# Float32 products for four units instead of eight, a fourth place for arriving weights, and x's first maximum spread in another bank

## The chip, the cores and the metric

The kernel runs on one core of a Trainium2 chip. The metric is the time of one execution on the device in microseconds (us), from the first to the last of its work; lower is better. The core's engines that appear here are TensorE (PE for its products, PEld for its weight loads), VectorE (DVE), ScalarE (ACT), GpSimd (POOL) and SyncE (SP), which in this kernel issues the transfers between HBM and the core's memory. PE writes its results into PSUM, in banks of 128 x 512 float32.

## The reference

Clustered attention over 4 batches, 8 heads, 768 positions and 64 columns a head, followed by a two-layer MLP on the result:

```python
q_assign = argmax(einsum('bhsd,hcd->bhsc', q_n, c_n))     # 16 clusters a head
k_assign = argmax(einsum('bhsd,hcd->bhsc', k_n, c_n))
scores = q @ k.T / sqrt(D), or -1e9 where q_assign != k_assign
attn = exp(scores - max(scores)); attn = attn / (sum(attn) + 1e-9)
x = (attn @ v) laid out as 3072 tokens x 512
h = x @ w_in                                              # 512 x 2048
g = s * relu(h)**2 + b
out = g @ w_out                                           # 2048 x 512
```

Everything comes and leaves in float32. The kernel does most products in float16, with a value split in a high and a low half (hi, lo) and three products added up.

## The kernel before

**Attention** is cut into 192 units, numbered in the order (b, c, hp, t, h): batch, a chunk of 256 positions, a pair of heads, a tile of 128 queries and a head of the pair. Four units share a chunk and pair of heads. For a unit, PE makes 128 x 768 scores (scores, L465), DVE takes the maximum (L475), ACT the exponential (exps, L482 and L485). The result p has to be transposed before it can be multiplied with the values. Up to unit 15 (TURN = 16) PE does this, three 128 x 128 pieces at a time (L509), into two PSUM banks that are called `turned` and that later hold the MLP's sums; from unit 16 on a transfer does it. Units 0 to 7 (RAW = 8) are copied out of the banks in float32, one half by DVE (L122) and one by ACT (L120), and multiplied with the values in float32 (L531). Units 8 to 15 are split: ACT writes the high part in float16 (L514), DVE subtracts it for the low part (L515), and 18 float16 products per unit follow (L536 to L538), in which the values are split too (prep_v). Units from 16 on are split before their transpose and multiplied at L563 to L565.

**x.** After four units, finish_x (L577) writes x split in two halves and has it transposed by a transfer. After the 16 units of a chunk of 256 tokens it takes x's maximum: DVE over the columns (L595), then allmax, in which PE spreads the 128 partitions' maxima over a bank (L98) and DVE reduces them (L99). The bank is the one of the tag m, of which there is one; the cluster products of later queries (`pq`, L396), and the values of the first 16 units (`px`), use it too.

**The weights.** w_in and w_out come as 32 pieces of 512 KB (fetch, L83 and L86), alternately wi and wo. They land in a tile with the tag stage, of which there are three. rebase (ACT, L204) and narrow (DVE, L208 and L209) turn the raw bits of a piece into a float32 tile and so free its place. bound (ACT, L216 or L218, with PE and DVE for wi) takes sums that bound the products. weights() holds these steps at a fixed distance: in round i, bound of piece i-3, rebase and narrow of i-2, fetch of i. When all pieces have been bounded, two scales follow (finish_w_in, finish_w_out), and wsplit makes float16 pairs of all weights (ACT L266, DVE L268), one step of the MLP after the other.

**The MLP** is 192 steps (b, c, ft): for each chunk of 256 tokens, 16 blocks of 128 hidden columns. A step is mlp_in (12 products, L620), mlp_relu (ACT: r, L627; g's high half, L629; the square, L630), mlp_gl (POOL, L635: g's low half) and mlp_out (6 products, L647). mlp_start makes a chunk's scales from x's maximum in seven small DVE operations (L602 to L611), the first L627 needs them. In the program the steps run 21 units behind the attention (LAG = 21).

**What sets the order.** The program is written unit by unit, with helpers that advance a step at a time. Each engine's order is then made by a scheduler, which puts an instruction where its own estimate and the priorities allow; `tc.high_priority(offset=300)` (first_of_all) lets the instructions under it move ahead, and is used for the first 20 units. On the chip each engine then runs its instructions in that order, and waits for each one's inputs and buffers.

Of the kernel before, what the change touches and what calls it, by code (L numbers as in the profile page):

```python
# [8 lines left out]
F16 = mybir.dt.float16  # L9
# [9 lines left out]
P = 128  # L19
# [7 lines left out]
def tile_cluster_attention_mlp(ctx, tc, q, k, v, cent, w_in, w_out, s_in, b_in, out):  # L27
# [15 lines left out]
    LAG = 21  # L43
    BIGN = 11

    RAW = 8
    TURN = 16
    URGENT = 20

# [43 lines left out]

    def allmax(dst, src, name, bank="m"):
        n = src.shape[1]
        pm = (ps_m if bank == "m" else ps_h).tile([P, 512], F32, tag=bank, name=f"am_{name}")
        for j in range(n):
            nc.tensor.matmul(pm[:, j * P : (j + 1) * P], src[:, j : j + 1].broadcast_to([P, P]), identb, start=True, stop=True)  # L98
        V.tensor_reduce(dst, pm[:, : n * P].rearrange("p (n q) -> p n q", q=P), axis=AX.X, op=ALU.max)  # L99
# [14 lines left out]
    G.tensor_copy(identb, ident)  # L114
    ones16 = const([P, P], F16, "ones16")
    G.memset(ones16, 1.0)

    def copy(eng, dst, src):
        if eng is A:
# [46 lines left out]
    wo = {}  # L166
    WSP = {}

    def weight_tile(name):
        return cp.tile([P, KT, P], F32, tag="w", name=name, bufs=2 * NF + 1)  # L170
    w1 = const([P, NF], F32, "w1")
# [18 lines left out]
    def fetch(p):  # L190
        ft = p // 2
        if p % 2 == 0:
            w = wi[ft] = weight_tile(f"wi{ft}")
            src = w_in.bitcast(I32)[:, ft * 2 * P : (ft + 1) * 2 * P].rearrange("(t p) f -> p t f", p=P)
        else:
            w = wo[ft] = weight_tile(f"wo{ft}")
            src = w_out.bitcast(I32)[ft * P : (ft + 1) * P, :].rearrange("p (a f) -> p a f", a=KT)
        st = sb.tile([P, KT, P, 2], I32, tag="stage", name=f"wst_{p}", bufs=3)
        load(st.rearrange("p a f w -> p a (f w)"), src)
        return {"w": w, "st": st, "p": p, "ft": ft}  # L200

    def rebase(d):
        hw = d["st"][:, :, :, 1].bitcast(F32)
        A.activation(d["w"], hw, AF.Prelu, scale=2.0 ** -112, alpha=-(2.0 ** 32))  # L204

    def narrow(d):
        c = d["w"].bitcast(I32)
        V.tensor_scalar(c, c, 3, None, op0=ALU.logical_shift_left)  # L208
        V.scalar_tensor_tensor(c.bitcast(U32), d["st"][:, :, :, 0].bitcast(U32), 29, c.bitcast(U32),  # L209
                               op0=ALU.logical_shift_right, op1=ALU.bitwise_or)  # L210
# [16 lines left out]

    def weights():
        live = {}
        for i in range(2 * NF + 3):  # L230
            if 0 <= i - 3:
                bound(live[i - 3])
                narrowed[0] += 1
            if 0 <= i - 2 < 2 * NF:
                rebase(live[i - 2])
                narrow(live[i - 2])
            if i < 2 * NF:
                live[i] = fetch(i)
            if i < 2 * NF + 2:
                yield  # L240

    def finish_w_in():
# [164 lines left out]
    def prep_v(b):  # L407
        vm = sb.tile([P, 8], F32, tag="vm", name=f"vm_{b}", bufs=2)
        VM[b] = vm
        vns = []  # L410
        for hp in range(NP):
            vn = sb.tile([P, 2, T, D], F32, tag="kv", name=f"vn_{b}_{hp}", bufs=5)
            load(vn, v[b, 2 * hp : 2 * hp + 2].rearrange("h (p t) d -> p h t d", t=T), False)
            vns.append(vn)
            if b == 0:
                VN[hp] = vn
            yield
        if b:
            yield from until(START[b][3])
        for hp in range(NP):  # L420
            absmax(vm[:, hp : hp + 1], vns[hp].rearrange("p h t d -> p (h t d)"))
            if hp < NP - 1:
                yield
        vc = columns(1, f"v{b}")
        V.tensor_reduce(vc, vm[:, 0:NP], axis=AX.X, op=ALU.max)
        if b:
            yield
        allmax(vm[:, 5:6], vc, f"v{b}")
        yield
        floor2(V, vm[:, 6:7], vm[:, 5:6])  # L430
        inverse2(V, vm[:, 7:8], vm[:, 6:7], 0)
        V.tensor_scalar(vm[:, 7:8], vm[:, 7:8], 2.0 ** 13, None, op0=ALU.mult)
        V.tensor_scalar(vm[:, 6:7], vm[:, 6:7], 2.0 ** -19, None, op0=ALU.mult)
        for hp in range(NP):
            vh = sb.tile([P, 2, T, D + 2], F16, tag="vh", name=f"vh_{b}_{hp}", bufs=5)
            vl = sb.tile([P, 2, T, D], F16, tag="vl", name=f"vl_{b}_{hp}", bufs=5)
            VS[(b, hp)] = (vh, vl)
            G.memset(vh[:, :, :, D:], 1.0)
            yield from split(vh[:, :, :, :D], vl, vns[hp], vm[:, 7:8], False)
            if hp < NP - 1:  # L440
                yield
                if b > 0:
                    yield from until(48 * b - 8 + 4 * hp)
# [133 lines left out]
    def finish_x(g):  # L577
        b, c, hp = units[4 * g][:3]
        xs = XT.pop(g)
        if 4 * g < RAW:  # L580
            A.activation(xs, xs, AF.Copy, scale=VM[0][:, 7:8])
        if hp == 0:
            XM[(b, c)] = sb.tile([P, 8], F32, tag="xm", name=f"xm_{g}", bufs=4)
        xn = sb.tile([P, CT, 2, 2, D], F16, tag="xn", name=f"xn_{g}", bufs=1)
        A.activation(xn[:, :, 0], xs, AF.Copy)
        absmax(XM[(b, c)][:, hp : hp + 1], xs.rearrange("p t h d -> p (t h d)"))
        yield
        G.tensor_tensor(xn[:, :, 1], xs, xn[:, :, 0], op=ALU.subtract)
        x = sb.tile([P, CT, 2, P], F16, tag="x", name=f"x_{g}", bufs=9)
        XS[(b, c, hp)] = x  # L590
        nc.sync.dma_start_transpose(x.rearrange("p t e q -> p (t e) q"), xn.rearrange("p t e h d -> p (t e h d)"))
        if hp == NP - 1:
            xm = XM[(b, c)]
            xc = columns(1, f"x{g}")
            V.tensor_reduce(xc, xm[:, 0:NP], axis=AX.X, op=ALU.max)  # L595
            allmax(xm[:, 5:6], xc, f"x{g}")


    MS = {}
# [23 lines left out]
    def mlp_relu(b, c, ft):  # L623
        n = f"{b}_{c}_{ft}"
        ph = GS[(b, c, ft)]
        r = sb.tile([P, CW], F32, tag="r", name=f"r_{n}", bufs=2)
        A.activation(r, ph[:, :CW], AF.Relu, scale=MS[(b, c)][0])  # L627
        g = sb.tile([P, 2, CW], F16, tag="g", name=f"g_{n}", bufs=4)
        A.activation(g[:, 0, :], r, AF.Square)  # L629
        A.activation(r, r, AF.Square)  # L630
        GS[(b, c, ft)] = (r, g)
# [54 lines left out]
        at(LAG - 4 + ft, wsplit(ft))  # L686
    wgen = weights()

    def first_of_all(k):
        return tc.high_priority(offset=300) if k < URGENT else nullcontext()  # L690

    def run(gen):
        for _ in gen:
            pass
# [41 lines left out]
    with behind(last_turn[0], *last_split):  # L736
        some(first_v, 1)
        sv = scalar_in(s_in, "sv")
        bv = scalar_in(b_in, "bv")
        some(wgen, 3)  # L740
    run(first_k[0])
    run(first_q[0])
    run(first_k[1])
# [2 lines left out]
    while i < NU + 8 or i - LAG < NS + 4:  # L746
# [21 lines left out]
                exps(i)  # L768
        if 0 <= m < NS:
            if steps[m][2] == 0:  # L770
                mlp_start(*steps[m][:2])
            mlp_in(*steps[m])
            mlp_relu(*steps[m])
        if 0 <= i - 1 < NU:
# [38 lines left out]
```

## Time and profile before

| | us |
|---|---|
| median of three runs | 953.33 (951.72 to 954.87) |
| the profiled execution | 951.04 |
| its span, first to last instruction | 949.3 |
| PE busy | 835.3 (88%) |
| ACT busy | 713.9 (75%) |
| DVE busy | 639.7 (67%) |
| POOL busy | 546.4 (58%) |

All times of single instructions are from the profiled execution, counted from the start of its span. The program falls into stages: up to about 36 us the first keys and queries are prepared, from about 24 to 122 us the weights arrive beside the first units, to about 161 us they are split, and from about 165 us on the MLP's steps run between the units. The units end near 880 us.

### The profile page before, as it was taken

What the parts mean: (1) busy time and instruction counts of PE and PEld (TensorE: products, weight loads), DVE (VectorE), ACT (ScalarE), POOL (GpSimd) and SP (SyncE); (2) the same over time, 40 slices, a digit from 0 to 9 for tenths busy, and PEclk for the clock granted to TensorE, in tenths of its full rate; (3) what the DMA queues carried; (4) which work ended last, traced back from release to release, by engine and by line L of the source; (5) the groups of instructions that cost most, each with busy time, mean ns of one, the idle gap of its engine ahead of it and who ended that gap; (6) DMA issues with size and microseconds to landing.
All of it is one profiled execution on the core that took longest, in us unless ns stands there. A gap on an engine that the chain in (4) does not pass through costs nothing. (4 is left out here: it accounts for less than half of the span.)

```text
span 949.3 us, 22900 instructions
## 1 busy us (share of the span) xinstructions
PE 835.3 (88%) x8673; PEld 586.3 (62%) x8673; DVE 639.7 (67%) x1680; ACT 713.9 (75%) x1406; POOL 546.4 (58%) x580
## 2 busy tenths in 40 slices
PE   0567566988999898999998999999999999999997
PEld 0356343656566566777676666666776667777664
DVE  7797888999577767667876766776686567654100
ACT  3476766777587777888887978887888788888443
POOL 3010114577576666778687667776776666676321
PEclk9967575899999899999999999999999999999999
DMA  6888813778787897969778877888978768575300
GB/s 174 219 215 242 225 38 78 181 141 145 160 157 146 178 200 132 181 150 180 157 173 151 198 181 147 160 146 185 180 160 167 145 129 165 125 161 114 46 23 23
DMA packets 437759, 144.25 MB, mean 152 GB/s; under 512 B 405392, under 2 KB 434064, under 8 KB 437648
## 3 DMA queue, kind: packets, MB, share of 16 engines
q1 hardware_dynamic: 437648, 142.78, 71.6%
q8 instruction: 68, 1.11, 0.5%
q14 instruction: 43, 0.35, 0.1%
HBM read 35.69 MB, written 6.29 MB: 44 GB/s over the span
## 5 line engine op out<-in xcount | busy, mean ns | idle before, releaser
L517 POOL TENSOR_TENSOR ph<-p,ph 128x768 f16<-128x768 f32 x176 | 298.5, 1696 | 92.8 <-ACT ph L120 53.8
L647 PE MATMUL acc<-wos,g 128*128 128x512 f16 x1152 | 299.8, 381 | 5.1 <-POOL g L635 4.6
L620 PE MATMUL h<-x,wis 128*128 128x256 f16 x2304 | 290.5, 275 | 5.1 <-DMA x<-xn 3.3
L620 PEld LDWEIGHTS <-wis 128*128 128x128 f16 x2304 | 220.5, 98 | 53.7 <-issue 6.7
L635 POOL TENSOR_TENSOR g<-r,g 128x256 f16<-128x256 f32 x192 | 135.0, 704 | 120.8 <-ACT r L630 100.7
L485 ACT ACTIVATE p<-sc,ssm,qsm 128x768 f32<-128x768 f32 x192 | 188.3, 981 | 2.1
L475 DVE TENSOR_REDUCE ssm<-sc 128x1 f32<-128x768 f32 x192 | 181.9, 948 | 6.9 <-PE sc L465 6.9
L647 PEld LDWEIGHTS <-g 128*128 128x128 f16 x1152 | 102.7, 98 | 82.3 <-POOL g L635 7.5
L627 ACT ACTIVATE r<-h,cf 128x256 f32<-128x256 f32 x192 | 89.6, 467 | 77.2 <-PE h L620 63.4
L120 ACT ACTIVATE ph<-p 128x768 f16<-128x768 f32 x164 | 136.4, 832 | 0.6
L482 ACT ACTIVATE ssm<-ssm,lift,qsm 128x1 f32<-128x1 f32 x192 | 73.0, 380 | 70.5 <-DVE ssm L475 68.9
L563 PE MATMUL sc<-vh,PT 128*128 128x65 f16 x1032 | 118.1, 196 | 7.0 <-DMA PT<-ph 6.8
L565 PE MATMUL sc<-vh,PT 128*128 128x65 f16 x1032 | 120.5, 194 | 0.0
L564 PE MATMUL sc<-vl,PT 128*128 128x64 f16 x1032 | 119.4, 193 | 0.0
L563 PEld LDWEIGHTS <-PT 128*128 128x128 f16 x1056 | 99.4, 98 | 26.4 <-DMA PT<-ph 13.7
L465 PE MATMUL sc<-KA,QA 128*128 128x384 f16 x384 | 99.7, 342 | 16.3 <-ACT p L485 12.8
L564 PEld LDWEIGHTS <-PT 128*128 128x128 f16 x1056 | 98.9, 100 | 12.0 <-issue 0.7
L465 PE MATMUL sc<-KB,QB 128*128 128x384 f16 x384 | 99.8, 343 | 6.2 <-DMA QB<-qb 6.2
L565 PEld LDWEIGHTS <-PT 128*128 128x128 f16 x1056 | 99.2, 98 | 1.3
L569 DVE TENSOR_SCALAR ssm<-sc 128x1 f32<-128x1 f32 x172 | 26.3, 153 | 93.8 <-PE sc L565 92.8
L629 ACT ACTIVATE g<-r 128x256 f16<-128x256 f32 x192 | 78.9, 411 | 2.7
L630 ACT ACTIVATE r<-r 128x256 f32<-128x256 f32 x192 | 78.7, 410 | 2.7
(172 smaller groups left out, 1134.7 us busy)
## 6 DMA issues: line engine op xcount, KB each, us to landing
wst<-in_moe_w_in_dram SPq DMA_DIRECT2D x16, 512.0 KB, 4.5
wst<-in_moe_w_out_dram SPq DMA_DIRECT2D x16, 512.0 KB, 4.8
kn<-in_k_dram SPq DMA_DIRECT2D x16, 384.0 KB, 3.9
qn<-in_q_dram SPq DMA_DIRECT2D x24, 256.0 KB, 3.3
vn<-in_v_dram SPq DMA_DIRECT2D x16, 384.0 KB, 4.1
out_dram<-o SPq DMA_DIRECT2D x12, 512.0 KB, 3.4
PT<-ph SPq DMA_TRANSPOSE x176, 3.4
x<-xn SPq DMA_TRANSPOSE x48, 2.7
```

The costliest lines, as they stand in the source:

```text
L120: A.activation(dst, src, AF.Copy)
L465: last_score[0] = nc.tensor.matmul(sc[:, e, :HALF], X[:, col, :], y[:, h * S + e * HALF : h * S + (e + 1) * HALF], start=st, stop=not st)
L475: last_max[0] = V.tensor_reduce(SM[i // 4][:, 0, j : j + 1], U[i]["sc"], axis=AX.XY, op=ALU.max, negate=True)
L485: last_exp[0] = A.activation(p.rearrange("p (a b) -> p a b", a=2), u["sc"], AF.Exp, bias=bi, scale=u["scale"], **total)
L517: G.tensor_tensor(u["ph"][:, 1, :], u["p"], u["ph"][:, 0, :], op=ALU.subtract)
L563: nc.tensor.matmul(o1, PT[:, kt, :], vh[:, h, kt, : D + 1], start=(kt == 0), stop=False)
L564: nc.tensor.matmul(o, PT[:, kt, :], vl[:, h, kt, :], start=False, stop=False)
L565: nc.tensor.matmul(o1, PT[:, T + kt, :], vh[:, h, kt, : D + 1], start=False, stop=(kt == T - 1))
L620: nc.tensor.matmul(ph[:, :CW], WSP[ft][0][:, wl, kt, :], XS[(b, c, kt)][:, :, xl, :], start=(i == 0), stop=(i == len(terms) - 1))
L627: A.activation(r, ph[:, :CW], AF.Relu, scale=MS[(b, c)][0])
L635: G.tensor_tensor(g[:, 1, :], r, g[:, 0, :], op=ALU.subtract)
L647: nc.tensor.matmul(acc[:, t, :], g[:, gl, rows], WSP[ft][1][:, wl, :], start=(ft == 0 and gl + wl == 0), stop=(ft == NF - 1 and gl == 1))
```

## The change

RAW goes from 8 to 4: units 4 to 7 are now split like units 8 to 15, and their values with them. The split of the first batch's values is written in the order of head pairs 1, 2, 3, 0, since pair 0's four units (0 to 3) are all in float32 now, and the work yields after each pair.

g's four buffers, until now a tag with four tiles, become one constant tile gs with four slots, used in turn (ft % 4). Before the MLP starts, this tile, 512 KB like a piece of the weights, is the place of every fourth piece (p % 4 == 3). So four pieces can be on their way: weights() fetches piece i when piece i-3 is narrowed and i-4 bounded, and four are fetched at the start.

The spreading of x's maximum for the first chunk takes the first of the `turned` banks in place of bank m, and this and the first mlp_start stand under first_of_all, which is moved up in the program and gets a second argument.

```diff
-    RAW = 8
+    RAW = 4
...
     def allmax(dst, src, name, bank="m"):
         n = src.shape[1]
-        pm = (ps_m if bank == "m" else ps_h).tile([P, 512], F32, tag=bank, name=f"am_{name}")
+        if bank == "turned":
+            pm = turned[:, 0]
+        else:
+            pm = (ps_m if bank == "m" else ps_h).tile([P, 512], F32, tag=bank, name=f"am_{name}")
...
+    def first_of_all(k, end=URGENT):
+        return tc.high_priority(offset=300) if k < end else nullcontext()
...
+    gs = const([P, 4, 2, CW], F16, "gs")
...
-        st = sb.tile([P, KT, P, 2], I32, tag="stage", name=f"wst_{p}", bufs=3)
+        if p % 4 == 3:
+            st = gs.rearrange("p n e q -> p (n e q)").bitcast(I32).rearrange("p (a f w) -> p a f w", a=KT, w=2)
+        else:
+            st = sb.tile([P, KT, P, 2], I32, tag="stage", name=f"wst_{p}", bufs=3)
         load(st.rearrange("p a f w -> p a (f w)"), src)
...
     def weights():
         live = {}
-        for i in range(2 * NF + 3):
-            if 0 <= i - 3:
-                bound(live[i - 3])
+        for i in range(2 * NF + 4):
+            if 0 <= i - 4:
+                bound(live[i - 4])
                 narrowed[0] += 1
-            if 0 <= i - 2 < 2 * NF:
-                rebase(live[i - 2])
-                narrow(live[i - 2])
+            if 0 <= i - 3 < 2 * NF:
+                rebase(live[i - 3])
+                narrow(live[i - 3])
             if i < 2 * NF:
                 live[i] = fetch(i)
-            if i < 2 * NF + 2:
+            if i < 2 * NF + 3:
                 yield
...
-        for hp in range(NP):
+        for hp in ((1, 2, 3, 0) if b == 0 else range(NP)):
...
-            if hp < NP - 1:
+            if b == 0 or hp < NP - 1:
                 yield
...
-            V.tensor_reduce(xc, xm[:, 0:NP], axis=AX.X, op=ALU.max)
-            allmax(xm[:, 5:6], xc, f"x{g}")
+            with first_of_all(b + c, 1):
+                V.tensor_reduce(xc, xm[:, 0:NP], axis=AX.X, op=ALU.max)
+                allmax(xm[:, 5:6], xc, f"x{g}", "m" if b + c else "turned")
...
-        g = sb.tile([P, 2, CW], F16, tag="g", name=f"g_{n}", bufs=4)
+        g = gs[:, ft % 4]
...
-        some(wgen, 3)
+        some(wgen, 4)
...
-                mlp_start(*steps[m][:2])
+                with first_of_all(m, 1):
+                    mlp_start(*steps[m][:2])
```

The engines' orders move at three places that the prediction speaks of. In the rows below a name's first numbers are those of the piece, unit or step, and the last is the tile's; the changed kernel's line numbers lie some ten lines further on (L496 is its exp, L639 its r).

First, SP near the start, with the first pieces of the weights (wst_0 to wst_2) and the transposes of the first queries and keys. Before:

```order
L83 DMA wst_0_257<-in_moe_w_in_dram 128x4x256
L161 DMA_TRANSPOSE cT_126<-cnat_120 128x3x128
L83 DMA wst_1_260<-in_moe_w_out_dram 128x1024
L83 DMA wst_2_266<-in_moe_w_in_dram 128x4x256
L387 DMA_TRANSPOSE QA_0_0_0_200<-qa_0_0_0_186 128x8x128
L350 DMA_TRANSPOSE KB_0_0_195<-kb_131 128x12x128
```

And now:

```order
L83 DMA wst_0_258<-in_moe_w_in_dram 128x4x256
L167 DMA_TRANSPOSE cT_126<-cnat_120 128x3x128
L83 DMA wst_1_261<-in_moe_w_out_dram 128x1024
L83 DMA wst_2_264<-in_moe_w_in_dram 128x4x256
L83 DMA gs_128<-in_moe_w_out_dram 128x1024
L398 DMA_TRANSPOSE QA_0_0_0_201<-qa_0_0_0_187 128x8x128
L361 DMA_TRANSPOSE KB_0_0_196<-kb_132 128x12x128
```

A fourth piece, into gs, stands ahead of QA's transpose.

Second, ACT at the end of the weights, up to the first split of a weight (wis0). wab is what bound writes; the last is wab_31. Before:

```order
L204 ACTIVATE wo15_1290<-wst_31_1291 128x512
L218 ACTIVATE wab_30_1364<-wi15_1254 128x512
L514 ACTIVATE PT_11_1106<-turned_134 128x384
L485 ACTIVATE p_13_1175<-sc_13_1168,ssm_12_1101,qsm_0_0_1_218 128x768
L216 ACTIVATE wab_31_1382,l1_129<-wo15_1290 128x512
L514 ACTIVATE PT_11_1106<-turned_134 128x384
L266 ACTIVATE wis0_1488<-wi0_256,glob_130 128x512
```

And now:

```order
L215 ACTIVATE wo15_1306<-gs_128 128x512
L227 ACTIVATE wab_29_1341,l1_130<-wo14_1217 128x512
L229 ACTIVATE wab_30_1412<-wi15_1298 128x512
L525 ACTIVATE PT_9_1020<-turned_135 128x384
L493 ACTIVATE ssm_12_1153<-ssm_12_1153,lift_133,qsm_0_0_1_219 128x1
L227 ACTIVATE wab_31_1430,l1_130<-wo15_1306 128x512
L525 ACTIVATE PT_10_1072<-turned_135 128x384
L496 ACTIVATE p_12_1156<-sc_12_1148,ssm_12_1153,qsm_0_0_1_219 128x768
L277 ACTIVATE wis0_1536<-wi0_257,glob_131 128x512
```

Before, the exp of unit 13 stood ahead of the last bound; now the exp of unit 12 stands behind it, and one more unit's work is left for the time behind the weights.

Third, ACT where the MLP starts: the first r. Before:

```order
L485 ACTIVATE p_20_1610<-sc_20_1578,ssm_20_1607,qsm_0_1_0_829 128x768
L266 ACTIVATE wos6_1934<-wo6_732,glob_130 128x512
L120 ACTIVATE ph_20_1677<-p_20_1610 128x768
L485 ACTIVATE p_21_1681<-sc_21_1651,ssm_20_1607,qsm_0_1_0_829 128x768
L266 ACTIVATE wis7_1939<-wi7_740,glob_130 128x512
L627 ACTIVATE r_0_0_0_1704<-h_0_0_0_1691,cf_0_0_1687 128x256
```

And now:

```order
L277 ACTIVATE wis4_1767<-wi4_558,glob_131 128x512
L277 ACTIVATE wos4_1824<-wo4_566,glob_131 128x512
L496 ACTIVATE p_19_1572<-sc_19_1563,ssm_16_1448,qsm_0_1_0_835 128x768
L639 ACTIVATE r_0_0_0_1751<-h_0_0_0_1738,cf_0_0_1734 128x256
L641 ACTIVATE gs_128<-r_0_0_0_1751 128x256
L493 ACTIVATE ssm_20_1655<-ssm_20_1655,lift_133,qsm_0_1_0_835 128x1
```

The first r moves from behind unit 21's exp to right behind unit 19's. On PE the product that spreads the maximum moves with it, from behind a cluster product and ahead of unit 22's scores to right behind the scores of unit 20. At unit 36 as many steps stand ahead of the unit's exp as before, at unit 44 one fewer, and towards the end the two orders are alike.

More of the change, by code (lines that the diff above doesn't have):

```diff
@@ L687, in tile_cluster_attention_mlp @@
     wgen = weights()
-    def first_of_all(k):
-        return tc.high_priority(offset=300) if k < URGENT else nullcontext()
     def run(gen):
```

## The prediction

> **What bounds the kernel now.** I read the page's totals and its chain of waits first, then cut the span into stages, and then asked in each stage which wait ends last.
>
> ```profile
> PE 835.3 (88%) x8673; PEld 586.3 (62%) x8673; DVE 639.7 (67%) x1680; ACT 713.9 (75%) x1406; POOL 546.4 (58%) x580
> PE 27%; DMA 2%; issue 2%; ACT 1%; POOL 1%; DVE 1%; POOLq 0%; DVEq 0%; ACTq 0%
> 0.00:36.00 36.00, 7.39 (x84) 4.16 (x84) 28.36 (x90) 13.41 (x23) 9.91 (x42) 1.00 0.67 173
> 36.00:75.00 39.00, 27.05 (x200) 21.11 (x201) 33.30 (x75) 28.21 (x59) 4.64 (x7) 0.75 0.91 242
> 75.00:124.00 49.00, 30.11 (x224) 23.70 (x222) 37.07 (x90) 36.22 (x77) 2.96 (x5) 0.64 0.75 210
> 124.00:135.00 11.00, 7.43 (x53) 4.75 (x51) 8.53 (x27) 6.25 (x12) 0.67 (x1) 0.85 0.15 37
> 135.00:161.00 26.00, 14.89 (x155) 10.62 (x155) 21.72 (x46) 15.68 (x27) 8.83 (x8) 0.61 0.27 61
> 161.00:236.00 75.00, 65.94 (x680) 44.85 (x681) 70.04 (x159) 59.26 (x116) 51.25 (x44) 0.91 0.71 151
> 236.00:265.00 29.00, 26.83 (x259) 17.27 (x257) 18.78 (x56) 17.73 (x33) 17.04 (x19) 1.00 0.84 153
> 265.00:600.00 335.00, 317.73 (x3535) 223.21 (x3532) 235.62 (x629) 269.14 (x528) 236.35 (x237) 0.99 0.84 168
> 600.00:880.00 280.00, 274.76 (x3049) 194.58 (x3046) 179.59 (x491) 237.35 (x466) 197.44 (x196) 1.00 0.77 152
> ```
>
> Each row of the table is one stretch: its length, then the busy time of PE, PEld, DVE, ACT and POOL, the granted TensorE clock, the DMA share and GB/s. From 265 to 880 PE is busy for 592.5 of 615 us (96%): the products bound those two thirds, and nothing in this change touches them. What it touches lies ahead of 265, where PE sits idle for 85 us (28.6 + 12.0 + 18.9 + 3.6 + 11.1 + 9.1 + 2.2). There DVE is the fullest engine: 85% in 36 to 75, 76% in 75 to 124, 84% in 135 to 161, 93% in 161 to 236. So the question is what holds the weights (36 to 124) and the first MLP step (after 161).
>
> The weights: 32 pieces of 512 KB come through three places.
>
> ```profile
> SPq L86 <- DVE wo L209: 22.7, 12, 3.8
> SPq L86 <- DVE wi L209: 19.1, 10, 3.3
> ACT wi L204 <- DMA wst<-in_moe_w_in_dram: 7.7, 6, 1.7
> ACT wo L204 <- DMA wst<-in_moe_w_out_dram: 4.1, 6, 1.3
> DMA to landing us min/median/max: 3.2/4.7/7.3
> L86 SPq DMA_DIRECT2D wst<-in_moe_w_out_dram x15: 341/345/1213, 39.8 to 115.9; - x15
> L208 DVE TENSOR_SCALAR wi<-wi x16: 407/420/428, 26.0 to 118.9; 128x512 int32<-128x512 int32 x16
> L209 DVE SCALAR_TENSOR_TENSOR wo<-wst,wo x16: 673/684/835, 27.8 to 122.0; 128x512 uint32<-128x512 uint32 x16
> 73.58 0.68 ACT L204 ACTIVATE wi<-wst 128x512 f32<-128x512 f32 x1 [1.14 <-DMA wst<-in_moe_w_in_dram]
> 120.84 0.66 ACT L204 ACTIVATE wo<-wst 128x512 f32<-128x512 f32 x1 [0.73 <-DMA wst<-in_moe_w_out_dram]
> ```
>
> The queue waits for DVE to read a place free (41.8 us over 0 to 161), and ACT waits for the piece (11.8 us in 75 to 124): a closed loop. Its round is issue 0.35, landing 4.7, L204 0.67, L208 0.42, L209 0.68, together 6.8 us; three places give 2.27 us a piece. Measured from piece 12 (73.58) to piece 31 (120.84): 47.26 / 19 = 2.49 us.
>
> The first MLP step waits for x's maximum:
>
> ```profile
> 149.94 0.16 DVE L595 TENSOR_REDUCE amb_x<-xm 128x1 bf16<-128x4 f32 x1
> 161.04 0.29 PE L98 MATMUL am_x<-identb,amb_x 128*128 128x128 bf16 x1 [1.52 <-DVE oe_q L288]
> 165.35 0.45 ACT L627 ACTIVATE r<-h,cf 128x256 f32<-128x256 f32 x1
> ```
>
> Its input is ready at 150.1, but the spreading product waits 10.9 us for bank m, which a cluster product's maximum (L287, L288) still reads; r then follows 4.3 us later.
>
> **The change part by part**, against the profiled execution's 951.04 us.
>
> *One fetch ahead of the first queries' transpose.* The fourth place's first fetch now stands ahead of the transpose of QA on SP.
>
> ```profile
> 25.39 0.67 ACT L204 ACTIVATE wo<-wst 128x512 f32<-128x512 f32 x1 [1.00 <-DMA wst<-in_moe_w_out_dram]
> 26.84 0.67 ACT L204 ACTIVATE wi<-wst 128x512 f32<-128x512 f32 x1 [0.79 <-DMA wst<-in_moe_w_in_dram]
> PE sc L465 <- DMA QA<-qa: 2.8, 1, 2.8
> ```
>
> Pieces that stream arrive 1.45 us apart, and the first scores do wait for QA (2.8 us), so I take +1.5, one piece's transfer; the bounds are 0 (the transpose overlaps it) and 1.8 (the same with 0.35 us of issue, from row L86 above).
>
> *Units 4 to 7 with split values.* Per unit, two copies become two subtractions on DVE behind two casts on ACT:
>
> ```profile
> L515 DVE TENSOR_TENSOR PT<-turned,PT x16: 544/549/558, 96.6 to 147.2; 128x384 f16<-128x384 f32 x16
> L122 DVE COPY PT<-turned x8: 541/548/557, 39.0 to 86.4; 128x384 f32<-128x384 f32 x8
> ```
>
> Before, DVE copied one half and ACT the other (e = 0 and 1); now DVE subtracts both: 4 x (2 x 0.549 - 0.548) = +2.2 us of DVE, ACT a little more beside it. On PE:
>
> ```profile
> L531 PE MATMUL px<-vn,PT 128*128 128x64 f32 x96 | 17.0, 342 | 0.0
> L536 PE MATMUL px<-vh,PT 128*128 128x65 f16 x48 | 8.4, 234 | 4.2 <-DVE xs L548 2.5 <-ACT PT L514 1.4 <-DVE oe_q L288 0.3
> L537 PE MATMUL px<-vl,PT 128*128 128x64 f16 x48 | 8.3, 232 | 0.0
> L538 PE MATMUL px<-vh,PT 128*128 128x65 f16 x48 | 8.0, 234 | 0.7 <-DVE PT L515 0.7
> ```
>
> Eight units took 17.0 us in float32 and eight took 24.7 us in float16, 3.1 against 2.1 a unit, so four cost 3.9 us more by these rows; PE has 18.9 us idle in 75 to 124, and I put this at nothing. Without that cover it would be 3.9 at most. In 36 to 75 DVE has 5.7 us free, which covers it in part; without that cover it costs all 2.2. I take +1.1, bounds 0 and 2.2.
>
> *The fourth place.* The same round of 6.8 us with four in flight would give 1.70 us a piece. But the DMA engines were 75% busy in those 49 us, so on each of the 19 pieces, with everything else that moved, they spent 0.75 x 49 / 19 = 1.93 us, and that is the floor at a full queue. The busiest stretch in the table has a share of 0.91; at that share the pace is 1.93 / 0.91 = 2.12 us. From 2.49 to 2.12 over 19 pieces: -7.0 us, which I take. Bounds: 0, and -11.9 (DVE's idle time in the stretch, 49 - 37.07; the floor of 1.93 gives -10.6). A stretch ahead of 75 already stands at 0.91 and gets nothing.
>
> Here the Trainium skill's page "DMA: Bandwidth & Descriptors", section "Specifications", would be kinder: it limits a core's HBM reads to about 358 GB/s, so 512 KB could pass in an estimated 1.46 us, in line with the 1.45 us between two streamed arrivals above; by it the loop's 1.70 us would stand and the term would be (2.49 - 1.70) x 19 = -15, more than DVE's idle time allows. The same page, section "Latency and other measured facts", speaks against the change: it gives an HBM access 0.2 us on average and 2 us under high load. If the fourth transfer brought that load, the round would be an estimated 8.6 us, 2.15 us a piece, and the term (2.27 - 2.15) x 19 = -2.3. No run so far has four in flight.
>
> *What falls behind the end of the weights.* ACT's order shows that the last bound of the weights now stands ahead of unit 12's exp; before, it stood behind unit 13's. So one unit moves out of the stretch.
>
> ```profile
> 122.30 0.98 ACT L485 ACTIVATE p<-sc,ssm,qsm 128x768 f32<-128x768 f32 x1
> 151.80 0.97 ACT L485 ACTIVATE p<-sc,ssm,qsm 128x768 f32<-128x768 f32 x1
> L475 DVE TENSOR_REDUCE ssm<-sc 128x1 f32<-128x768 f32 x192 | 181.9, 948 | 6.9 <-PE sc L465 6.9
> ```
>
> These are the exps of units 13 and 19: 29.5 / 6 = 4.92 us a unit. The weights stretch loses that unit's DVE work, 0.95 + 2 x 0.55 = 2.05 us. Net +2.9; bounds 0 (its work is done in the idle time anyway) and 4.9.
>
> *The first maximum in the transposes' banks, first of all.* PE's product moves from behind a cluster product to right behind unit 20's scores, and mlp_start's seven small DVE operations get priority. r of step 0 moves from behind the exps of units 20 and 21 to right behind unit 19's: by 165.35 - (150.1 + 4.3) = 10.9 us at most. PE can then fill its 11.1 us of idle time in 135 to 161 with about three steps.
>
> ```profile
> L647 PE MATMUL acc<-wos,g 128*128 128x512 f16 x1152 | 299.8, 381 | 5.1 <-POOL g L635 4.6
> L620 PE MATMUL h<-x,wis 128*128 128x256 f16 x2304 | 290.5, 275 | 5.1 <-DMA x<-xn 3.3
> 239.44 0.49 PE L620 MATMUL h<-x,wis 128*128 128x256 f16 x3 [1.86 <-DMA x<-xn]
> ```
>
> A step is (299.8 + 290.5) / 192 = 3.07 us of PE, so three are 9.2 us. Two things hold most of it back. In 161 to 236 DVE has only 75 - 70.04 = 5.0 us free, and its work for the units is not less; and step 16 waits for the next four units' x (239.44), so steps run ahead only wait there. In PE's new order the lead of two to three steps at units 20 to 31 is gone at unit 36. I take -3.0, a little over half of DVE's 5.0, since a start 10.9 us earlier is twice what is needed to reach it; bounds 0 and -9.2. With the transposes' banks the new product waits for unit 15's last reading of them, which ends at about 147.7 (row L515 above), so that is no new wait.
>
> *The rest.* g's four slots, now fixed, are four buffers as before; a weight piece leaves the last of them by 122, long before the first r. The order of the V splits and first_of_all's new place add no instruction. From 265 on PE is bound as before: 0, within 2 us either way.
>
> The sum: +1.5 + 1.1 - 7.0 + 2.9 - 3.0 = -4.5, so 946.5 for a profiled execution. The one shown lies 953.33 - 951.04 = 2.3 us under the median of the runs; with that, 948.8.
>
> **The rivals.**
>
> A, *a larger gain.* The weights go at the floor of 1.93 us (-10.6), the extra subtractions vanish in idle time (0), and the MLP's lead takes all of DVE's 5.0 us: 1.5 + 0 - 10.6 + 2.9 - 5.0 = -11.2, so 942.1 on the median. For it: DMA's and DVE's idle time in 75 to 124 (12.3 and 11.9 us) would bear it. Against: both would have to be used to the end at once, and ACT has 36.2 of 49 us there too. The Trainium skill's limit of an HBM read, cited above, would be on this side; DVE's idle time caps it here.
>
> B, *the MLP's lead is given back.* At unit 36 the order has the steps where they were, and at unit 44 one step later; then the last term is 0: 1.5 + 1.1 - 7.0 + 2.9 = -1.5, so 951.8: no change that can be told. If the fourth place does less than it says, because the queue's transposes keep the pace, it ends here too, on the upper side (the fourth place's term at -5: 953.8). For it: PE's own order. Against: 161 to 236 has 9.1 us of idle PE.
>
> C, *the fourth transfer only waits longer: slower.* Landing lengthens with what is in flight: the rows show 3.2 to 7.3 us. Four places give no better pace than three once the round is 4 x 2.27 = 9.1 us, that is, once the median landing is 7.0 us or more. Then the fourth place's term is 0, the subtractions cost all, and the late unit all: 1.5 + 2.2 + 0 + 4.9 - 3.0 = +5.6, so 958.9. For it: a share of 0.91 in 36 to 75. Against: 0.75 and ACT waiting in 75 to 124, and arrivals 1.45 us apart when pieces stream. A landing that lengthens by less, to 6.3 us, say, halfway, leaves (2.27 - 8.4 / 4) x 19 = -3.2 in the fourth place's term and ends with B's upper side. The Trainium skill's latency under load, cited above, is a reason for this rival, and no more than that: its 1.8 us do not reach the 2.3 us from which it decides.
>
> **How the numbers follow.** What can be told from no change is 0.3%, 2.9 us: faster is under 950.5, slower over 956.2. The forecast (944.5 to 950.5) has 0.40, A 0.18, B 0.22, C 0.20. Forecast and A are faster, 0.58; B is the same, with a little of C's lower end, 0.24; slower is the rest, 0.18. The range goes from just under A's 942.1 to most of the way to C's 958.9: 941.0 to 957.5. For the gaining cases alone it would be 941 to 950.5.
>
> **What would show it.** The distance between the pieces' L204 in 75 to 124, 2.49 us now: 2.12 bears out the fourth place's term, 2.27 or more with landings of 7 us is C. The exp of unit 12 ahead of wis0's split, and the first split some four us earlier. QA's first landing 1.5 us later and the first scores with it. The first r at 4 to 5 us behind amb_x, not 15, and PE's idle time in the 25 us ahead of the first r down from 11 us. The x of unit group 7, which step 16 waits for at 239.44: at about 235 it is the forecast, at 228 A, at 238 B, at 245 C. From there the two traces should run in parallel; if the distance changes by over 3 us between there and the end, my reading that the rest is untouched is wrong.

## The result and the profile after

The changed kernel took 947.83 us (median of 20 runs, 945.01 to 952.97), beside 952.88 for the kernel before, measured beside it (20 runs, 947.14 to 961.22): a ratio of 0.995, 95% interval 0.9933 to 0.9966. Run again in a later session, it gave 0.9944 (0.9923 to 0.9965). So it is 5 us faster, give or take 1.6 in the first session and 2.0 in the second; forecast were 4.5.

The page's totals and the stages, first of the profile of the change (its execution took 952.97 us; columns as in the table before):

```profile
PE 830.0 (87%) x8697; PEld 580.1 (61%) x8697; DVE 651.1 (68%) x1684; ACT 715.4 (75%) x1405; POOL 548.0 (58%) x580
0.00:36.00 36.00, 5.91 (x80) 3.73 (x80) 28.84 (x91) 14.59 (x26) 9.90 (x42) 1.00 0.64 177
36.00:75.00 39.00, 24.78 (x189) 18.59 (x189) 30.67 (x68) 25.07 (x48) 4.31 (x6) 0.77 0.98 263
75.00:124.00 49.00, 31.46 (x284) 23.36 (x285) 42.68 (x107) 40.24 (x86) 3.84 (x5) 0.66 0.62 190
135.00:161.00 26.00, 18.16 (x189) 12.33 (x186) 22.38 (x49) 17.44 (x31) 13.13 (x12) 0.74 0.28 62
161.00:236.00 75.00, 59.34 (x623) 39.84 (x621) 66.71 (x149) 56.06 (x110) 49.65 (x43) 0.97 0.70 152
265.00:600.00 335.00, 317.22 (x3518) 222.79 (x3516) 242.22 (x631) 267.66 (x526) 233.28 (x235) 0.99 0.83 166
600.00:880.00 280.00, 272.69 (x3020) 193.19 (x3017) 180.57 (x490) 235.64 (x460) 196.41 (x194) 1.00 0.77 151
```

In 36 to 75 the DMA engines went from a share of 0.91 to 0.98 and from 242 to 263 GB/s (the row of the change's second profile stands below); DVE's busy time in 75 to 124 rose from 37.1 to 42.7 us; PE did 18.2 instead of 14.9 us in 135 to 161. From 265 on the rows are as before.

```profile
36.00:75.00 39.00, 25.07 (x189) 18.76 (x189) 30.84 (x69) 25.32 (x48) 4.30 (x6) 0.77 1.01 263
```

The weights in the first of the change's profiles: the landing of a piece, the queue's waits for a free place (over 0 to 150), ACT's casts of pieces 12 and 31, and the wait of the first scores for QA:

```profile
DMA to landing us min/median/max: 3.7/5.3/7.7
SPq L86 <- DVE wi L220: 21.6, 10, 6.1
SPq L86 <- DVE wo L220: 13.9, 7, 4.4
66.63 0.66 ACT L215 ACTIVATE wi<-wst 128x512 f32<-128x512 f32 x1 [1.92 <-DMA wst<-in_moe_w_in_dram]
110.74 0.67 ACT L215 ACTIVATE wo<-gs 128x512 f32<-128x512 f32 x1
PE sc L476 <- DMA QA<-qa: 4.1, 1, 4.1
```

A landing takes 5.3 us instead of 4.7 (5.5 in the second profile), far from the 7.0 at which four places would be worth no more than three. The last piece is cast at 110.7 instead of 120.8.

The first maximum, its spreading, and the first r:

```profile
145.22 0.16 DVE L607 TENSOR_REDUCE amb_x<-xm 128x1 bf16<-128x4 f32 x1
146.46 0.31 PE L101 MATMUL turned<-identb,amb_x 128*128 128x128 bf16 x1
151.18 0.46 ACT L639 ACTIVATE r<-h,cf 128x256 f32<-128x256 f32 x1
```

The product waits 1.1 us where it waited 10.9; the first r follows the maximum by 6.0 us, not 15.4.

One profile of a kernel is not enough here: the execution profiled before (951.04) lies under the median of its kernel, that of the change (952.97) is the slowest of its 20. So both kernels were profiled once more, and the table has all four. Times are starts in us; what has one instruction a unit or step is named by its number in the order.

| | before, 951.04 | before, 960.27 | change, 952.97 | change, 949.78 |
|---|---|---|---|---|
| exp of unit 0 | 36.9 | 37.3 | 39.3 | 38.8 |
| cast of piece 12 | 73.6 | 74.4 | 66.6 | 66.4 |
| cast of piece 31, the last | 120.8 | 122.5 | 110.7 | 111.8 |
| first split of a weight | 124.6 | 126.2 | 116.9 | 117.9 |
| exp of unit 16 | 137.4 | 139.2 | 134.9 | 135.4 |
| exp of unit 20 | 161.1 | 162.9 | 158.6 | 159.1 |
| first r | 165.4 | 167.1 | 151.2 | 151.7 |
| last products into h of step 16 | 239.7 | 243.7 | 242.6 | 242.9 |
| exp of unit 48 (MLP steps begun) | 295.8 (28) | 301.0 (28) | 291.9 (27) | 292.1 (27) |
| exp of unit 100 (all at 79 steps) | 513.7 | 519.3 | 513.1 | 512.7 |
| exp of unit 191, the last | 877.0 | 886.8 | 879.5 | 876.3 |

Mean against mean, the change is 10.4 us ahead at the last cast, 3.2 at unit 16 and at unit 20, 6.4 at unit 48 with a step fewer done (so 3.3, at 3.07 us a step), 3.6 at unit 100 (with as many steps begun, but mlp_out done for 78 and not 76 of them) and 4.0 at unit 191. The gain is there at unit 16 and still there at the end; in between it depends on what one counts as done.

### The profile page after: what moved, and what is told of

The parts are those of the page before. It is cut to its first block, busy times and chain, and to the rows that moved or that the text cites. A ratio compares the mean times of both kernels' runs of the same rounds, so it can differ in the third digit from the quotient of the medians.

```text
span 951.3 us, 22936 instructions
## 1 busy us (share of the span) xinstructions
PE 830.0 (87%) x8697; PEld 580.1 (61%) x8697; DVE 651.1 (68%) x1684; ACT 715.4 (75%) x1405; POOL 548.0 (58%) x580
## 4 chain that ended last, share of the span: by engine, by line
PE 45%; DVE 23%; DMA 12%; ACT 7%; issue 5%; POOL 2%; SPq 1%; POOLq 0%; DVEq 0%; ACTq 0%
PE h L632 16%; PE acc L659 16%; PE sc L476 6%; DVE ssm L486 5%; DMA qn<-in_q_dram 3%; DMA PT<-ph 2%; PE sc L574 2%; DMA kn<-in_k_dram 2%; DMA vn<-in_v_dram 2%; PE sc L576 2%; PE sc L575 2%; ACT p L496 1%; DVE wis L279 1%; DVE qa L196 1%; DMA wst<-in_moe_w_in_dram 1%
## 5 line engine op out<-in xcount | busy, mean ns | idle before, releaser
L528 POOL TENSOR_TENSOR ph<-p,ph 128x768 f16<-128x768 f32 x176 | 297.0, 1688 | 129.7 <-ACT ph L126 71.1
L632 PE MATMUL h<-x,wis 128*128 128x256 f16 x2304 | 291.9, 276 | 16.1 <-ACT r L639 9.7
L659 PE MATMUL acc<-wos,gs 128*128 128x512 f16 x1152 | 299.7, 381 | 4.1 <-POOL gs L647 2.8
L496 ACT ACTIVATE p<-sc,ssm,qsm 128x768 f32<-128x768 f32 x192 | 188.5, 982 | 2.0
L647 POOL TENSOR_TENSOR gs<-r,gs 128x256 f16<-128x256 f32 x192 | 136.5, 712 | 88.1 <-ACT r L642 79.4
L659 PEld LDWEIGHTS <-gs 128*128 128x128 f16 x1152 | 101.4, 98 | 79.4 <-POOL gs L647 5.6
L639 ACT ACTIVATE r<-h,cf 128x256 f32<-128x256 f32 x192 | 89.2, 465 | 57.8 <-PE h L632 54.5
L574 PE MATMUL sc<-vh,PT 128*128 128x65 f16 x1032 | 117.4, 195 | 6.9 <-DMA PT<-ph 6.8
L576 PE MATMUL sc<-vh,PT 128*128 128x65 f16 x1032 | 117.9, 193 | 0.0
L575 PEld LDWEIGHTS <-PT 128*128 128x128 f16 x1056 | 98.5, 99 | 11.8 <-issue 0.5
L641 ACT ACTIVATE gs<-r 128x256 f16<-128x256 f32 x192 | 78.9, 411 | 2.7
```

The lines of the kernel that those rows point to most:

```text
L496: last_exp[0] = A.activation(p.rearrange("p (a b) -> p a b", a=2), u["sc"], AF.Exp, bias=bi, scale=u["scale"], **total)
L528: G.tensor_tensor(u["ph"][:, 1, :], u["p"], u["ph"][:, 0, :], op=ALU.subtract)
L574: nc.tensor.matmul(o1, PT[:, kt, :], vh[:, h, kt, : D + 1], start=(kt == 0), stop=False)
L575: nc.tensor.matmul(o, PT[:, kt, :], vl[:, h, kt, :], start=False, stop=False)
L576: nc.tensor.matmul(o1, PT[:, T + kt, :], vh[:, h, kt, : D + 1], start=False, stop=(kt == T - 1))
L632: nc.tensor.matmul(ph[:, :CW], WSP[ft][0][:, wl, kt, :], XS[(b, c, kt)][:, :, xl, :], start=(i == 0), stop=(i == len(terms) - 1))
```

## The experiments

Three parts can be there or not: the fourth place (F), the split of units 4 to 7 with the new order of the values' splits (R), and the maximum's bank with its priority (K). All eight combinations were run; in all but the kernel before, g has its four fixed slots (gs) and first_of_all its new place, which by themselves were not timed. My theory is the sum of the prediction: F -2.6 (the late unit counted with it), R +1.1, K -3.0. The rivals are that one of F and K carries everything and the other is given back.

**The change again.** 

> The changed kernel once more, so that its parts have a time from the same chip and its second profile can be laid beside the first, whose execution (952.97 us) lies at the slow end of its own runs. By both theories below: 5 us under the kernel before (0.993 to 0.997). If the loss of some 4 us that the first profile shows between 390 and 590 us belongs to that one execution, it is not in this profile; if it belongs to the order, it is here too.

0.9944 (0.9923 to 0.9965), median 948.27. The loss between 390 and 590 us is not in this profile (step 48's r at 386.1 and step 96's at 587.0, where the first had 385.9 and 589.6): it belonged to the one execution.

**Without the fourth place.** weights(), the fetches at the start and the stage tag as before:

```diff
-        if p % 4 == 3:
-            st = gs.rearrange(...)
-        else:
-            st = sb.tile([P, KT, P, 2], I32, tag="stage", name=f"wst_{p}", bufs=3)
+        st = sb.tile([P, KT, P, 2], I32, tag="stage", name=f"wst_{p}", bufs=3)
...
-        some(wgen, 4)
+        some(wgen, 3)
```

> The change without its fourth place: three places for weight pieces and weights() as before; units 4 to 7 split, the first maximum in the transposes' bank. Theory 1 (my sum: the fourth place carries the gain, 1.5 - 7.0 + 2.9 = -2.6, the bank -3.0, the split +1.1): 1.9 us under before. Theory 2 (the early MLP start carries it all, since what the weights gain is given back at the wait for the next x): 5 us under before, like the whole change, with the last piece's cast near 120 us. Theory 3 (the fourth place carries it all, the early start is given back at that same wait): at or 1 us over before.

1.0017 (0.9993 to 1.0041): 1.6 us over before. Near theory 3; theory 2 is out, since with the early first r (157.7) the time is no shorter than before, and the 1.9 us under before of theory 1 lie outside the interval too.

**Without the split.**

```diff
-    RAW = 4
+    RAW = 8
...
-        for hp in ((1, 2, 3, 0) if b == 0 else range(NP)):
+        for hp in range(NP):
...
-            if b == 0 or hp < NP - 1:
+            if hp < NP - 1:
```

> The change with units 4 to 7 left in float32 and the split of the values in the order before. Theory 1: the split costs 1.1 us on DVE, so this is 5.6 to 6 us under before and 1 us under the change. Theory 2 and 3 say nothing of it. A rival: DVE is 91% busy where the weights arrive in the profile of the change, so the split work costs its full 2.2 us and this is 2 us under the change. If float32 products hold PE instead, it is over the change by up to 2 us.

0.9978 (0.9955 to 1.0002): 2.1 us under before, and 0.34% over the change in the same session, with an uncertainty of some 0.3% on that difference. Neither of the first two; the last possibility has the sign, with more than its size.

**Without the bank and the priority.**

```diff
-            with first_of_all(b + c, 1):
-                V.tensor_reduce(xc, xm[:, 0:NP], axis=AX.X, op=ALU.max)
-                allmax(xm[:, 5:6], xc, f"x{g}", "m" if b + c else "turned")
+            V.tensor_reduce(xc, xm[:, 0:NP], axis=AX.X, op=ALU.max)
+            allmax(xm[:, 5:6], xc, f"x{g}")
...
-                with first_of_all(m, 1):
-                    mlp_start(*steps[m][:2])
+                mlp_start(*steps[m][:2])
```

> The change with x's first maximum in bank m and without the priority of it and of mlp_start; four places and split units stay. Theory 1: the early start is worth 3.0 us, so this is 1.5 to 2 us under before. Theory 2: as before, within 1 us. Theory 3: 5 us under before, like the whole change, with the first r back at 15 us behind amb_x.

0.9985 (0.9963 to 1.0006): 1.4 us under before, nearest to theory 1. Theory 3's 5 us are out; theory 2's value, the time of before, lies within the interval, and it is the run without the fourth place that speaks against that theory. The rows of this run show the old wait:

```profile
142.46 0.16 DVE L606 TENSOR_REDUCE amb_x<-xm 128x1 bf16<-128x4 f32 x1
155.15 0.29 PE L101 MATMUL am_x<-identb,amb_x 128*128 128x128 bf16 x1 [1.30 <-DVE oe_q L299]
160.61 0.46 ACT L638 ACTIVATE r<-h,cf 128x256 f32<-128x256 f32 x1
```

**The fourth place alone** (the two edits before this one together). 

> The kernel before with the fourth place alone. Measured so far: the change without the fourth place is 1.6 us over before, without the split 2.6 and without the bank 1.9 us under it, the whole change 5.1 under. If the three parts add up, this is -6.9 (whole minus without) plus what is left over: between 4 and 7 us under before. If the fourth place needs the other parts (the time it gains is only kept where the split takes work off PE's float32 products or the early start uses it), it is 0 to 2 us under before.

0.9968 (0.9941 to 0.9996): 3.1 us under before. That lies between the two readings' ranges, 4 to 7 and 0 to 2, and decides neither.

**The bank and the priority alone.** 

> The kernel before with x's first maximum in the transposes' bank and its priority alone. Adding up: 3.5 us under before. My sum: 3.0 us under. If the early start is used only where the weights end earlier, 0 to 1 us under.

1.0005 (0.9978 to 1.0032): nothing, as the third reading has it. The first r came at 155.5 instead of 165.4, and x's transposes still held step 16 (its last products at 240.6).

**The split alone.** 

> The kernel before with units 4 to 7 split and the values' new order alone. My sum put the split at +1.1, with 0 and +2.2 as bounds. The run without it says the split is worth -2.5 us beside the other two parts. If that is its own worth (PE or the granted clock gains from the float32 products that fall away), this is 2.5 us under before; if my sum is right and the -2.5 comes from the other parts, 1 to 2 us over.

1.0086 (1.0053 to 1.0118): 8.2 us over before, far beyond every value offered. Its casts of pieces 12 and 31:

```profile
71.74 0.67 ACT L212 ACTIVATE wi<-wst 128x512 f32<-128x512 f32 x1
124.64 0.67 ACT L212 ACTIVATE wo<-wst 128x512 f32<-128x512 f32 x1
```

That is (124.64 - 71.74) / 19 = 2.78 us a piece. The eight together, with the same pace, the start of the last cast, and the number of units whose exp ACT starts between the casts of pieces 12 and 31, from each profile:

| | ratio to before | us | us a piece | last cast | units between |
|---|---|---|---|---|---|
| none (before) | 1 | 0 | 2.49, 2.53 | 120.8, 122.5 | 5, 5 |
| F | 0.9968 | -3.1 | 2.23 | 107.8 | 5 |
| R | 1.0086 | +8.2 | 2.78 | 124.6 | 7 |
| K | 1.0005 | +0.5 | 2.50 | 120.6 | 5 |
| F, R | 0.9985 | -1.4 | 2.21 | 108.0 | 5 |
| F, K | 0.9978 | -2.1 | 2.25 | 107.7 | 5 |
| R, K | 1.0017 | +1.6 | 2.88 | 124.7 | 7 |
| F, R, K (the change) | 0.9944 | -5.3 | 2.32, 2.39 | 110.7, 111.8 | 5, 5 |

With three places the pieces come 0.3 to 0.4 us further apart when the split is there; with four it costs them at most 0.15. My reading is an interaction that the sum did not have: where a place comes back only after DVE, and the loop is what is waited for, work added to DVE lengthens the loop. That is not shown. The two slow versions are also the two in which the scheduler has put seven units between the casts and not five, so more work was done in that time. And at the exp of unit 16 the split alone is at 138.8, level with the kernel before (137.4 and 139.2). Its profiled execution (960.21) is the fastest of its eight and ends like the second one before (both have the exp of unit 191 at 886.8), so where the 8.2 us of the medians arise cannot be read off it.

Averaged over the four pairs that differ in one part, F is worth -0.58% (-5.5 us), R +0.20% (+1.9) and K -0.24% (-2.3). Each ratio is known to some 0.25%, so these averages to some 0.18% or 1.7 us, if the ratios' errors are independent; R and K by themselves are hardly beyond that.

**A lighter second step of narrow**, in the change and in the kernel before. Three quarters of the weights keep zeros in their lowest three bits; that work is left out.

```diff
-        V.scalar_tensor_tensor(c.bitcast(U32), d["st"][:, :, :, 0].bitcast(U32), 29, c.bitcast(U32),
+        V.scalar_tensor_tensor(c[:, :1].bitcast(U32), d["st"][:, :1, :, 0].bitcast(U32), 29, c[:, :1].bitcast(U32),
```

> The change with the second step of narrow (DVE, 0.68 us a piece) done on a quarter of each piece: three quarters of the weights keep their lowest three bits at zero, so this leaves out work and only its time is of interest. It takes about 0.5 us of DVE off each piece. If DVE's work now sets the pace of the weights (busy 0.87 to 0.91 of the time from piece 4 to piece 31, at 2.3 to 2.4 us a piece), the pace falls by nearly all of the 0.5, to about 1.9, and the last cast comes some 10 us earlier than 111. If the loop of four places or the transfers set it, the round of 7.4 us (with the landing of 5.3) loses 0.5, which is 0.13 us a piece: 2.2, the last cast at 107.

0.9993 (0.9966 to 1.002). The pace is 2.25 us, the last cast at 107.3, and DVE's share from piece 4 to 31 falls from 0.87 or 0.90 to 0.79: nearer to what the loop has (2.2, 107) than to what DVE's work would give (1.9), though with 11 instead of 12 exps ahead of the last cast the order is not the same either. But the whole is 4 us slower than the change, with less to do. At unit 48 it is level with it (292.3, one step more done); between unit 48 and unit 191 it needs 590.1 us, with a step fewer left, where the change needed 587.7 and 584.3.

> The kernel before with the same lighter second step of narrow (the same work is left out). The loop of three places sets its pace by my reading, with DVE busy 0.83 of the time: the round of 6.8 us loses 0.5, 0.17 us a piece, so 2.3 instead of 2.49, the last cast near 116. If DVE's work sets it here too, the pace falls by 0.5, to 2.0.

0.9944 (0.992 to 0.9967), 5.3 us under before, but not by the pieces: their pace is 2.74, with 15 instead of 13 exps ahead of the last cast at 121.5. The scheduler spent DVE's free time on the units and not on the weights; unit 12 came at 104.9 instead of 112.6. My expectation of 2.3 had the order as given. So the loop cannot be all that sets the pace: what the scheduler puts between two pieces counts too.

**The fourth fetch behind the first transposes.**

```diff
-        some(wgen, 4)
+        some(wgen, 3)
     run(first_k[0])
     run(first_q[0])
     run(first_k[1])
+    with behind(last_turn[0], *last_split):
+        some(wgen, 1)
```

> The change with the first fetch into the fourth place moved behind the first transposes of queries and keys on SP. My sum priced its place ahead of them at +1.5; the first exps lie 1.9 to 2.4 us behind before's in the two profiles of the change. If that time is kept, this is 1.5 us under the change and the first exp near 37; if the start only shifts work that is not on the path, it is as the change, within 1 us.

0.9924 (0.9897 to 0.995), 7.3 us under before. The wait of the first scores is back at what it was before, and the first exp at 37.2:

```profile
PE sc L476 <- DMA QA<-qa: 2.8, 1, 2.8
PE sc L476 <- DMA QB<-qb: 1.8, 1, 1.8
```

The last cast still comes at 108.9. By its ratio this is the fastest version of all that keep the work whole, and faster than before; that it beats the change (0.995 and 0.9944) is not shown, since the intervals overlap.

**The bank without the priority.**

```diff
-            with first_of_all(b + c, 1):
...
-                with first_of_all(m, 1):
```

> The change with x's first maximum in the transposes' bank, but without the priority of it and of mlp_start. If the bank is what the wait was for (10.9 us in the profile before, put down to bank m), the first r stays within 6 us of amb_x and the time stays as the change's, within 1 us. If the order is what matters, the product goes back behind the cluster product, the first r to 10 us or more behind amb_x, and the time to that of the run with bank m, 3 us over the change.

The rows say the bank:

```profile
145.48 0.16 DVE L606 TENSOR_REDUCE amb_x<-xm 128x1 bf16<-128x4 f32 x1
146.14 0.22 PE L101 MATMUL turned<-identb,amb_x 128*128 128x128 bf16 x1
153.02 0.45 ACT L638 ACTIVATE r<-h,cf 128x256 f32<-128x256 f32 x1
```

The product follows in 0.5 us and the first r 7.5 us behind the maximum, 1.5 us later than in the change, and as late as in the version before this one, which has the priority. And yet the time is 1.0124 (1.0088 to 1.016), 11.8 us over before and 17 over the change. At unit 48 it stands at 293.3 with as many steps done as the change (292.1): the loss comes later. PE's busy time in 300 to 880, first here, then in the run without the split:

```profile
300.00:880.00 580.00, 544.51 (x5984) 382.44 (x5982) 376.89 (x1033) 459.56 (x901) 393.63 (x393) 0.99 0.80 156
```

```profile
300.00:880.00 580.00, 556.63 (x6173) 392.82 (x6170) 385.14 (x1052) 475.91 (x931) 404.68 (x405) 1.00 0.80 159
```

PE has 12 us more of idle time. From unit 60 to unit 191 this version takes 556.6 us and the run without the split 541.2, although from unit 60 on the two have the same instructions in the same order on all engines, waiting for the same things; the instructions take equally long (means, POOL's L528 1.68 us in both, the exp 0.98). The distance grows in small steps, at waits for QA, PT and the exps. What sets it off is open: an earlier state that the two don't share, at unit 60 a distance of 4.3 us, is all that I see. The profile does not show where in memory the tiles lie, so a difference in that is not ruled out. Of this version's six runs the profiled one is the slowest (970.04, median 965.61).

**The kernel before again.** 

> The kernel before once more, for a second profile of it: the first belongs to an execution of 951.04 us, some 3 us under the median of all its executions (953 to 955), while both profiles of the change belong to executions over their median of 948. If the first profile was early by luck in the first 300 us, this one has its exp of unit 48 at 298 or later, 6 us behind the change's 292, and the gain is made there; if the luck was in the later part, unit 48's exp is again near 296, and from unit 60 to unit 191 it needs some 587 us instead of 583.5.

957.07 us (8 runs) beside 956.14 of the kernel before in the same session (9 runs): 1.0, 0.9968 to 1.0032, as must be. Unit 48's exp comes at 301.0, and unit 60 to unit 191 takes 539.0 us beside 533.5: so the first profile was early in both parts, some 5 us in each. The 583.5 and 587 us of my expectation were wrong numbers for that stretch.

## Why the prediction was right

The time was right (948.8 forecast, 947.8 and 948.3 measured), the likeliest case came, and in the mean over the four pairs the three parts have the signs that the sum gave them. Not all of its steps were right. F, with its late unit, was priced at -2.6 and is worth -5.5 in that mean; and one by one the three parts add up to +5.6 us, not to -4.5. That a plain sum came within a microsecond of a change whose parts act on each other is in part luck.

*One fetch ahead, +1.5.* Right as to the wait: QA is waited for 4.1 instead of 2.8 us, 1.3 more, and with the fetch behind the transposes the wait is back at 2.8. The first exp comes 1.9 us later (mean of two) and 1.8 us of that are gone with the later fetch; but in the three profiles of F, of F and R, and of F and K, which have the fetch ahead too, it starts at 37.5 to 37.7, only about half a microsecond behind before's 36.9 and 37.3. So what the place in the queue costs the start lies between about 0.4 and 1.9.

*The split, +1.1, between 0 and 2.2.* In the mean over the four pairs +1.9, within the bounds; by itself +8.2, and beside F and K -3.2, both outside. What failed is that the term was given one price, whatever stands beside it. I put half of it at nothing because DVE has idle time in 36 to 75, and the runs neither bear that out nor refute it: the pieces of the split alone come 2.78 instead of 2.49 us apart, but with two more units among them. With four places, as in the change, the pieces hardly notice. That PE pays nothing for it was borne out: its busy time went from 835.3 to 830.0 us, and in each of the four pairs it is lower with the split, by 1.7 to 7.5 us (means, where there are two profiles), although the rows of L531 to L538 made it 3.9 more at most.

*The fourth place, -7.0.* The mechanism was right, its place was not. After piece 12 the pace went from 2.49 to 2.32 and 2.39, not to 2.12: -3.2 and -1.9 against the first profile before. But I had said that the stretch ahead of 75 would get nothing, since its DMA share stood at 0.91. It got most: piece 12 came 7.5 us earlier (mean of two), at a share of 0.98 and, in the second profile, 1.01. A share of 0.91 was not a full queue. The order does not explain this: piece 4 is cast at 46.7 and 46.5 us (before 46.9 and 47.1), and from there to piece 12 four units start their exps in both kernels. The two errors together left 10.4 us at the last cast.

The landing of a piece rose from 4.7 to 5.3 and 5.5 us with four in flight. Rival C, which needed 7.0, is out by these rows. The Trainium skill's rule on the latency of an HBM access (page "DMA: Bandwidth & Descriptors", section "Latency and other measured facts"), 0.2 us on average and 2 us under high load, had spoken against the change. The rise of 0.6 and 0.8 us is less than half of the 1.8 us, an estimate, that I had worked out from that rule.

*A unit behind the end of the weights, +2.9.* Right in kind: 12 exps instead of 13 lie ahead of the last cast. But the unit had fallen behind early and not at the end: ahead of piece 4 there are 3 exps instead of 4. Of the 10.4 us, 3.2 were left at unit 16, so 7.2 went to the later start and the units that were put off; my three terms for it came to 5.5.

*The first maximum, -3.0.* The bank's wait fell from 10.9 to 1.1 us and the first r came 14.8 us earlier (mean of two); in the mean over the four pairs this was worth -2.3. That the gain would be held at the wait for the next four units' x held too: step 16's last products start at 242.6 and 242.9 us, before at 239.7 and 243.7. But I had named x of group 7 at about 235 as the sign of the forecast and 238 as that of rival B; it landed at 239.3 and 239.8 (before 239.4 and 243.5), and the forecast came true all the same. The sign was wrong: it tells when x lands, and not how much has been done by then. Two more of its signs did not come either. PE's idle time in the 25 us ahead of the first r was to fall from 11 us, and it is 11.6 and 13.1 (before 10.8 in both profiles). And the distance between the two kernels was to change by no more than 3 us from the wait for x to the end: by the means the change is 1.1 us behind at step 16's last products and 4.2 ahead at the end of the span. Part of that is again what has been done: at these products the change has started 38 exps and the kernel before 37. The first split of a weight came 8.0 us earlier (means), where some four were named.

*The rest, 0.* Right as to this change: from unit 48 to unit 191 it takes 587.7 and 584.3 us with one step more to do, so 584.6 and 581.2, where the kernel before took 581.2 and 585.8. But the reason given was not: nothing of the change lies there, and yet the order does not stay. By the start of unit 100's exp, for one, PE has done mlp_out for 76 steps before and for 78 in the change; I had compared the order at a few units only. The lighter narrow and the bank without priority show what that term can be: the second lost 17 us against the change in a part of the program that its edit does not touch.

Rival A (-11.2) failed on the pace of the pieces. Rival B's mechanism, the steps' lead that is lost at unit 36, fits K alone (+0.5), but not the change. That F, R and K give more together than one by one, as the table has it, is shown by the times. Why is not: for R the loop of three places is my reading and two more units among the pieces are the rival, and why K is worth nothing alone or beside F, but 6.6 us beside R and 3.9 beside both, is not settled.

## What to carry to other kernels

A loop of transfers through a few places can be priced from everything that stands between a landing and the place's return, and that is where to look for what one more place is worth: the last piece came 10.4 us earlier in the change, and over the four pairs the place was worth 5.5. Work added on the engine that frees a place may cost the loop too; that is an idea to test, with the order held, and was not shown here. A DMA share of 0.91 in a stretch was no reason to give up on it: it went to 0.98. Where a scheduler makes the order, an edit of the first 150 us can move the last 700; parts must be timed together as well as alone, and a gain of half a per cent needs more than one profile of each kernel.

## What the runs showed that I had not expected

Two versions with the same order of instructions from unit 60 on took 541.2 and 556.6 us from there to the last unit, and a version with less work (the lighter narrow in the change) took 4 us more than the one with all of it. The profiled executions of one and the same kernel lay 9.2 us apart (951.04 and 960.27), 5.2 of it at the exp of unit 48.
